# A fused attention and feed-forward kernel: weight tiles decoded in pairs, in alternating operations, one pair a unit behind the gate's second remainder

## The chip, the cores and the metric

The kernel runs on one core of a Trainium2 chip. The metric is the device time of one execution in microseconds. Before the change it is 1063.06 us, the median of three runs (1061.4 to 1063.42).

The core has five engines with a queue each, and a queue runs in order: TensorE (PE in the rows; its weight loads are PEld), VectorE (DVE), ScalarE (ACT), GpSimd (POOL) and SyncE (SP), which here only issues DMAs. TensorE writes to PSUM, which has eight banks; the other engines evacuate them.

## The reference

Attention with a causal mask and a memory term, over 4 batches, 8 heads, 576 positions and 64 channels, gives 2304 tokens of 512 channels. Two feed-forward blocks follow:

```python
def _moe_ref(x, w_in, w_out):          # d_ff = 2048
    h = x @ w_in
    sp = np.where(h > 20.0, h, np.log1p(np.exp(np.minimum(h, 20.0))))
    g = h * np.tanh(sp)
    return (g @ w_out).astype(np.float32)

def _moe2_ref(x, w1, w2, w3, w_out):   # d_ff = 1024
    a = x @ w1
    b = x @ w2
    h = a * b @ w3
    return (h @ w_out).astype(np.float32)
```

The weights lie in DRAM as 64-bit floats.

## The kernel before

**Precision.** Each float32 operand of the feed-forward blocks is held as a rounded high part and a remainder, so a product is three matmuls: high by high, high by remainder, remainder by high.

**Decoding weights.** A weight tile of 128 by 512 is loaded as pairs of 32-bit words into a buffer `draw` (512 KB, line 94) and made into float32 by `decode` (lines 91 to 109): six VectorE operations on the whole tile, each on the result of the one before, at lines 99, 100, 101, 103, 104 and 105, and one GpSimd addition at line 108, which leaves the float32 tile in a buffer `da`. Then either `split_w` (line 114) rounds it on GpSimd (`pool_round`, line 64) and subtracts for the remainder (line 67, on GpSimd), both into the weight slot, or `split_to_dram` (line 119) writes both parts over the `draw` buffer and stores them to DRAM (line 126). The number of `draw` and `da` buffers is set by `decoder(stack, raw, n)`: 3 and 2 in the gated block, 2 and 2 from its last quarter on.

**Stages.** Attention comes first, some 0 to 290 us, for 16 pairs of heads; ten tiles are decoded beside it. The gated block (`_moe_ref`) follows in 24 units `u = (g, n)`: four quarters g of the 2048 columns, six chunks n of 384 tokens, loop at line 607. A unit does `emit_h(u)` (line 410 on: 48 matmuls into four PSUM banks, tanh, arctan and sine on ScalarE, and the gate product at line 443 on VectorE), then `emit_x2` of the unit before (line 523: 48 matmuls into the three `X` banks in four groups of 12; each group is evacuated by VectorE at line 537 or added to `x2` at line 539), then `split_y(u)` (line 446: high parts `gh` on ScalarE, two remainders `gl` on VectorE), whose VectorE instructions `tc.issue_after` queues behind the last evacuation of `emit_x2`. In the quarters before the last, the unit then decodes tiles: of the next quarter's weights (`load_quarter`, eight tiles, into one of two slots `wq0` and `wq1`), and of `predecode`, which puts the halves of three later weights into DRAM (16 tiles). Two `load_quarter` tiles come in units 0 and 1 of a quarter and one in each other; one `predecode` tile comes in most units from 1 on (lines 628, 629).

In the last quarter `fold` (line 544) multiplies w3 by the last output weight, in 16 steps that each decode one tile of w3 and transpose it on TensorE (line 563); its buffers take the place of the decoder's. The last stage (`emit_ab`, `emit_out`, about 755 us to the end) needs the second halves of w1 and w2: eight tiles decoded by `second_half` (line 149), two beside the last `emit_x2` and two behind each of the steps k = 0, 1 and 2.

**Order.** The program is written as generators; `steps(gen, n)` runs n steps of one. A planner then orders each engine's queue by simulated times, earlier in the program first among what is ready. An instruction without an edge to others may so move past what stands before it in the program.

Of the kernel before, what the change touches and what calls it, by code (L numbers as in the profile page):

```python
# [2 lines left out]

# [18 lines left out]
def fused_kernel(ctx: ExitStack, tc, q, k, v, M_prev, z_prev, beta, w_in, w_out, w1, w2, w3, w_out2, out):  # L22
# [65 lines left out]
    def dec_tile(tag):  # L88
        return dec["pool"].tile([128, dec["w"]], F32, tag=tag, name=tag, bufs=dec["n"])

    def decode(src):

        r = dec["pool"].tile([128, dec["w"], 2], I32, tag="draw", name="draw", bufs=dec["raw"])
        dm(out=r.rearrange("p n t -> p (n t)"), in_=src)
        lw, hw = r[:, :, 0], r[:, :, 1]
        a = dec_tile("da")
        ai, e = a.bitcast(I32), lw.bitcast(F32)
        V = nc.vector
        V.tensor_scalar(out=ai, in0=hw, scalar1=0x7FFFFFFF, scalar2=None, op0=ALU.bitwise_and)  # L99
        V.tensor_scalar(out=a, in0=a, scalar1=2.0 ** -15, scalar2=122879.9921875, op0=ALU.max, op1=ALU.min)  # L100
        V.tensor_scalar(out=ai, in0=ai, scalar1=3, scalar2=0x3FFFFFF8,  # L101
                        op0=ALU.logical_shift_left, op1=ALU.bitwise_and)
        V.scalar_tensor_tensor(out=ai, in0=hw, scalar=-0x40000000, in1=ai, op0=ALU.bitwise_and, op1=ALU.bitwise_or)  # L103
        V.tensor_scalar(out=hw, in0=ai, scalar1=-0x800000, scalar2=None, op0=ALU.bitwise_and)  # L104
        V.scalar_tensor_tensor(  # L105
            out=e, in0=lw.bitcast(U32), scalar=2.0 ** -52, in1=hw.bitcast(F32), op0=ALU.mult, op1=ALU.mult
        )
        nc.gpsimd.tensor_tensor(out=a, in0=a, in1=e, op=ALU.add)  # L108
        return a, r.rearrange("p n t -> p (n t)").bitcast(F32)

    def words(w, r0, c0):
        return w[r0:r0 + 128, c0:c0 + dec["w"]].bitcast(I32)

    def split_w(hi, lo, src):
        a, _ = decode(src)
        pool_round(hi, a)
        sub(lo, a, hi, nc.gpsimd)

    def split_to_dram(dst, src):

        a, r = decode(src)
        w = dec["w"]
        hi, lo = r[:, 0:w], r[:, w:2 * w]
        pool_round(hi.bitcast(F32R), a)
        nc.gpsimd.tensor_tensor(out=lo.bitcast(F32R), in0=a, in1=hi, op=ALU.subtract)
        dm(out=dst.rearrange("i p c -> p i c"), in_=r.rearrange("p (i c) -> p i c", i=2))


    ident = const.tile([128, 128], F32, name="ident")
    make_identity(nc, ident)  # L130
# [12 lines left out]
    def predecode():  # L143
        for w, wd in ((w_out2, o2_dram), (w1, w1_dram), (w2, w2_dram)):
            for c in range(w.shape[0] // 128):
                split_to_dram(wd[:, 128 * c:128 * c + 128, 0:WN], words(w, 128 * c, 0))
                yield

    def second_half(t):
        for i, w in ((1, w2), (0, w1)):  # L150
            for c in range(KD):
                split_w(t[:, i, 0, c], t[:, i, 1, c], words(w, 128 * c, WN))
                yield

    xl = {}

# [9 lines left out]
    def load_quarter(g):  # L166
        t = (wq if g % 2 == 0 else w2q[0]).tile([128, 2, KD + KQ, FQ], F32R, tag=f"wq{g % 2}", name="wqt")
        wts[g] = t
        for c in range(KD):
            split_w(t[:, 0, c], t[:, 1, c], words(w_in, 128 * c, FQ * g))  # L170
            yield
        for c in range(KQ):
            split_w(t[:, 0, KD + c], t[:, 1, KD + c], words(w_out, FQ * g + 128 * c, 0))
            yield

    w2q = [None]

# [268 lines left out]
    def split_y(u, y):  # L446
        gg = []
        for i in range(2):
            gh = wps[0].tile([128, 2, CH], F32R, tag="gh", name="gh", bufs=2)
            gl = wps[0].tile([128, 2, CH], F32R, tag="gl", name="gl", bufs=2)  # L450
            nc.scalar.copy(out=gh, in_=y[i])  # L451
            sub(gl, y[i], gh)
            gg.append((gh, gl))
        gt[u] = gg

    wk = ExitStack()
    wps = [None]
# [8 lines left out]
    for p in range(NPAIR + 1):  # L466

        now, old, new = p < NPAIR, p > 0, p + 1 < NPAIR
        if old:
            ensure_x((p - 1) // (2 * NP))  # L470
        if not now:
            ek.close()
            wps[0] = wk.enter_context(tc.tile_pool(name="wp", bufs=1, side="right"))
        if now:
            s_blocks(p, (3,))
        if old:
            for i in (4, 2, 3):
                pt_g(p - 1, i)
        if new:
            prep_qk(p + 1)  # L480
        if now:
            s_blocks(p, (2,))
            if p == 0:
                prep_phi(0)
            s_blocks(p, (0, 1))
        if p + 2 < NPAIR:
            load_pair(p + 2)
        if old:
            pt_g(p - 1, 5)
            if not now:  # L490
                steps(lq0, 100)
                split_y((0, 0), emit_h((0, 0)))
            pt_g(p - 1, 6)
        if now:
            normed(p, [(i, e) for e in range(2) for i in range(4)])
            pt_g(p, 1)
        if 2 <= p < 12:
            steps(background, 1)
# [45 lines left out]
    def fold():  # L544
        o2 = wq.tile([128, 2, 8, DM], F32R, tag="wq0", name="o2")
        oh, ol = o2[:, 0], o2[:, 1]
        for h in range(2):
            for i in range(2):
                dm(
                    out=f(o2[:, i, 4 * h:4 * h + 4]),  # L550
                    in_=o2_dram[i, 512 * h:512 * h + 512].rearrange("(k p) f -> p k f", p=128),
                )

        held = None
        po = None
        fp = fpool[0]
        for s in range(2 * (FF2 // 128) + 1):
            pt = None
            if s < 2 * (FF2 // 128):
                a, _ = decode(words(w3, 128 * (s // 2), 512 * (s % 2)))  # L560
                pt = psF()
                for j in range(4):
                    nc.tensor.transpose(pt[:, 128 * j:128 * j + 128], a[:, 128 * j:128 * j + 128], ident)
            if held is not None:
                n, th, tl = held
                m, g = n // 2, n % 2
                if g == 0:
                    po = psF()
                for j in range(4):
                    kk = 4 * g + j  # L570
                    mm(po, th[:, j], oh[:, kk], kk == 0, False)
                    mm(po, th[:, j], ol[:, kk], False, False)
                    mm(po, tl[:, j], oh[:, kk], False, kk == 7)
                if g == 1:
                    for h in range(2):
                        cs = slice(256 * h, 256 * h + 256)
                        wo = fp.tile([128, 256], F32, tag="wo", name="wo", bufs=1)
                        nc.scalar.copy(out=wo, in_=po[:, cs])
                        dm(out=w_dram[128 * m:128 * m + 128, cs], in_=wo)
            held = None  # L580
            if pt is not None:
                th = fp.tile([128, 4, 128], F32R, tag="w3h", name="w3h", bufs=1)
                tl = fp.tile([128, 4, 128], F32R, tag="w3l", name="w3l", bufs=1)
                pw = pt.rearrange("p (a b) -> p a b", b=128)
# [15 lines left out]
        return t  # L600

    folding = fold()
    pre0 = iter(())
    nextq = iter(())
    prev = None
    w1t, w2t = [None, None], [None, None]
    for u in [(g, n) for g in range(NQ) for n in range(NCH)]:
        g, n = u
        last = g == NQ - 1
        if u not in gt:  # L610
            if last and fpool[0] is None:
                steps(nextq, 100)
                steps(pre, 100)
# [5 lines left out]
            w_slot(0)  # L619
        if prev is not None:  # L620
            with tc.issue_after(emit_x2(prev, folding if last and n > 0 else pre0)):
                split_y(u, y)
        if last and n == 0:
            steps(folding, 1)
        if not last:
            if n == 0:
                nextq = load_quarter(g + 1)
            steps(nextq, 2 if n < 2 else 1)
            steps(pre, 1 if n in (1, 3, 4, 5) or (g < 2 and n == 2) else 0)
        prev = u  # L630
    NM = FF2 // 128

# [2 lines left out]
    for s in range(4):  # L635
# [1 line left out]
            out=f(wft[:, 1, 2 * s:2 * s + 2]),  # L637
            in_=w_dram[256 * s:256 * s + 256, :].rearrange("(k p) f -> p k f", p=128),
        )
    rest = second_half(w_slot(1))  # L640
    emit_x2(prev, rest)
    wk.close()


# [59 lines left out]
    split_x2(0)  # L704
    for k, (c, m) in enumerate(work):
        if k == 4:
            steps(rest, 100)
            fk.close()
            late = ctx.enter_context(tc.tile_pool(name="late", bufs=1))
            x2s = late.tile([128, 2, KD, 512], F32R, name="x2s")  # L710
# [46 lines left out]
```

## Time and profile before

| | |
|---|---|
| median of three runs | 1063.06 us |
| profiled execution, its own time | 1061.77 us |
| its span | 1060.0 us |
| TensorE busy | 1021.9 us (96%) |
| VectorE busy | 662.6 us (63%) |
| ScalarE busy | 502.5 us (47%) |
| GpSimd busy | 349.4 us (33%) |

The profiled execution lies 1.3 us under the median and within the three runs; 1.8 us of it lie outside the span. Times of rows are counted from the span's start. A busy time is the sum of an engine's instructions in a stretch. Matmuls overlap, so the length of one says less than the distance between two or the time of a row of them.

### The profile page before, as it was taken

How to read it: one execution, taken by the hardware profiler on the slowest of the kernel's cores; microseconds unless marked ns; L12 is line 12 of the kernel's file. 1: busy time of each engine (PE TensorE's matmuls, PEld its weight loads, DVE VectorE, ACT ScalarE, POOL GpSimd, SP SyncE). 2: the span in 40 equal slices, each digit the busy share in tenths (PEclk: the TensorE clock that was granted, in tenths of full speed). 3: DMA queues.
4: the chain of work that ended last, by engine and by line, in shares of the span. 5: the costliest groups of instructions: out<-in, count | busy, mean ns of one | idle time of the engine just before them, and what ended most of it. 6: DMA issues, size and time to landing. Idle time of an engine off the chain costs nothing.

```text
span 1060.0 us, 15074 instructions
## 1 busy us (share of the span) xinstructions
PE 1021.9 (96%) x5552; PEld 852.3 (80%) x5552; DVE 662.6 (63%) x1364; ACT 502.5 (47%) x1016; POOL 349.4 (33%) x345
## 2 busy tenths in 40 slices
PE   7999999999989899799979999999989999999998
PEld 4555655656789899799979999999868888888897
DVE  5999998854699847994887566566994112121111
ACT  4777867866654565346545643544323122211212
POOL 6776666632265515541553112011550000000000
PEclk9999999999999899999999999999999999999999
DMA  6434344310223301331132156222410010100101
GB/s 149 112 96 114 92 106 112 88 31 3 100 99 121 120 20 45 135 130 50 40 124 96 41 204 228 75 80 70 159 60 1 1 40 1 41 0 1 41 1 60
DMA packets 93626, 81.73 MB, mean 77 GB/s; under 512 B 68720, under 2 KB 72816, under 8 KB 93552
## 3 DMA queue, kind: packets, MB, share of 16 engines
q1 hardware_dynamic: 93552, 80.76, 24.6%
q8 instruction: 44, 0.72, 0.3%
q14 instruction: 30, 0.25, 0.1%
HBM read 65.54 MB, written 15.20 MB: 76 GB/s over the span
## 4 chain that ended last, share of the span: by engine, by line
PE 71%; DVE 18%; POOL 4%; issue 2%; DMA 2%; ACT 2%; SPq 1%; POOLq 0%; DVEq 0%; ACTq 0%
PE psX L61 27%; PE psA L61 25%; PE psF L61 12%; PE psF L385 4%; PE psX L266 2%; DVE da L99 2%; DVE da L100 2%; DVE da L103 2%; DVE draw L104 2%; DVE draw L105 2%; DVE da L101 2%; DVE y L443 1%; POOL da L108 1%; DVE gl L67 1%; POOL wqt L67 1%
## 5 line engine op out<-in xcount | busy, mean ns | idle before, releaser
L61 PE MATMUL psX<-gh,wqt 128*128 128x384 f32 x768 | 200.2, 342 | 17.0 <-DVE x L539 11.4
L108 POOL TENSOR_TENSOR da<-da,draw 128x512 f32<-128x512 f32 x72 | 106.2, 1476 | 289.3 <-DVE draw L105 250.9
L61 PEld LDWEIGHTS psX<-gh,wqt 128*128 128x128 f32 x768 | 141.3, 192 | 20.4 <-DVE x L539 12.8
L61 PE MATMUL psX<-gl,wqt 128*128 128x384 f32 x384 | 130.1, 341 | 0.8 <-DVE gl L67 0.6
L61 PE MATMUL psA<-xt,wqt 128*128 128x384 f32 x624 | 117.3, 338 | 2.1 <-DVE y L443 2.1
L61 PEld LDWEIGHTS psA<-xt,wqt 128*128 128x128 f32 x624 | 110.4, 190 | 3.9 <-DVE y L443 2.4
L337 ACT ACTIVATE s<-s,acc 128x384 f32<-128x384 f32 (+3 forms) x144 | 85.0, 595 | 37.5 <-DVE acc L332 21.0
L61 PE MATMUL psA<-x2h,w12t 128*128 128x512 f32 (+1 forms) x288 | 80.7, 355 | 4.2 <-POOL w12t L64 3.5
L451 ACT CAST gh<-y 128x768 fp32r<-128x768 f32 x48 | 40.1, 837 | 92.0 <-PE psX L61 46.6
L61 PE MATMUL psX<-wft,room 128*128 128x512 f32 x336 | 82.6, 390 | 0.0
L99 DVE TENSOR_SCALAR da<-draw 128x512 int32<-128x512 int32 x72 | 44.5, 619 | 53.8 <-issue 12.9
L332 DVE CUSTOM_DVE_ANT_0 s<-psA,mask 128x512 f32<-128x512 f32 (+2 forms) x144 | 64.9, 478 | 19.8 <-PE psA L61 17.2
L681 ACT COPY bs<-psA 128x512 f32<-128x512 f32 (+1 forms) x40 | 21.8, 544 | 113.5 <-PE psA L61 105.5
L61 PE MATMUL psX<-pt,raw 128*64 128x64 f32 (+4 forms) x576 | 75.0, 328 | 0.0
L61 PEld LDWEIGHTS psX<-gl,wqt 128*128 128x128 f32 x384 | 73.6, 192 | 1.6 <-DVE gl L67 1.4
L61 PE MATMUL psA<-kt,qt 64*128 64x384 f32 (+3 forms) x256 | 71.0, 485 | 3.4 <-DVE acc L332 2.8
L61 PE MATMUL psF<-xt,wqt 128*128 128x384 f32 x408 | 74.0, 335 | 0.0
L61 PEld LDWEIGHTS psX<-wft,room 128*128 128x128 f32 x336 | 62.6, 188 | 12.7
L387 ACT COPY pt<-psF 128x512 f32<-128x512 f32 (+1 forms) x112 | 59.0, 544 | 26.9 <-PE psF L385 23.4
L61 PEld LDWEIGHTS psF<-xt,wqt 128*128 128x128 f32 x408 | 70.9, 188 | 0.4 <-DVE y L443 0.3
L61 PE MATMUL psA<-x2s,w12t 128*128 128x512 f32 x288 | 67.9, 389 | 0.0
L682 DVE TENSOR_TENSOR bs<-bs,psA 128x512 f32<-128x512 f32 (+1 forms) x20 | 12.7, 633 | 87.3 <-PE psA L61 87.3
(117 smaller groups left out, 2022.6 us busy)
## 6 DMA issues: line engine op xcount, KB each, us to landing
draw<-in_moe_w_dram SPq DMA_DIRECT2D x32, 512.0 KB, 3.7
draw<-in_moe_w_out_dram SPq DMA_DIRECT2D x24, 512.0 KB, 3.7
draw<-in_moe_w_in_dram SPq DMA_DIRECT2D x16, 512.0 KB, 3.9
out_dram<-ob SPq DMA_DIRECT2D x18, 256.0 KB, 2.0
raw<-in_q_dram SPq DMA_DIRECT2D x32, 128.0 KB, 2.7
raw<-in_k_dram SPq DMA_DIRECT2D x32, 128.0 KB, 3.2
raw<-in_v_dram SPq DMA_DIRECT2D x32, 128.0 KB, 2.7
o_dram<-draw SPq DMA_DIRECT2D x8, 512.0 KB, 2.8
```

Source lines behind the costliest of these rows:

```text
L61: nc.tensor.matmul(o, lhsT=l, rhs=r, start=start, stop=stop)
L67: return (eng or nc.vector).tensor_tensor(out=dst, in0=src, in1=f(hi), op=ALU.subtract)
L99: V.tensor_scalar(out=ai, in0=hw, scalar1=0x7FFFFFFF, scalar2=None, op0=ALU.bitwise_and)
L100: V.tensor_scalar(out=a, in0=a, scalar1=2.0 ** -15, scalar2=122879.9921875, op0=ALU.max, op1=ALU.min)
L101: V.tensor_scalar(out=ai, in0=ai, scalar1=3, scalar2=0x3FFFFFF8, op0=ALU.logical_shift_left, op1=ALU.bitwise_and)
L108: nc.gpsimd.tensor_tensor(out=a, in0=a, in1=e, op=ALU.add)
L332: nc.vector.tensor_tensor_reduce(out=s, in0=o, in1=m, op0=ALU.add, op1=ALU.min, scale=-scale, scalar=init, accum_out=a,)
L337: nc.scalar.activation(out=s, in_=s, func=AF.Exp, scale=-1.0, bias=a, accum_out=r)
L385: nc.tensor.transpose(o[:, 128 * x:128 * x + 128], src[:, 128 * jb:128 * jb + 128], ident)
L387: nc.scalar.copy(out=t[:, 0:n], in_=o[:, 0:n])
L451: nc.scalar.copy(out=gh, in_=y[i])
L681: nc.scalar.copy(out=bs, in_=pb)
```

## The change

`decode` takes a list of sources and gives the six VectorE operations for all of them in turns: the first operation of each tile, then the second of each, and so on; the GpSimd addition and what follows is done tile by tile. `load_quarter`, `predecode` and `second_half` now yield jobs, a source and what is to be done with the decoded tile, and `run(jobs, n)` decodes n of them together. In the gated block a unit runs one pair behind `split_y`, which returns its second remainder; `tc.issue_after(split)` queues the pair's VectorE instructions behind it. Unit 0 of a quarter takes two `predecode` tiles (four in unit (0, 0)), units 1 to 3 take two tiles of the next quarter, units 4 and 5 one of each kind. `second_half` goes in pairs at its old places, the first pair at the start of the last `emit_x2`. In attention a single tile is run at a time as before, and so in `fold`.

```diff
+    def decode(srcs):
+        V = nc.vector
+        ts = []
+        for src in srcs:
+            r = dec["pool"].tile([128, dec["w"], 2], I32, tag="draw", name="draw", bufs=dec["raw"])
+            dm(out=r.rearrange("p n t -> p (n t)"), in_=src)
+            a = dec_tile("da")
+            ts.append((r[:, :, 0], r[:, :, 1], a, a.bitcast(I32), r.rearrange("p n t -> p (n t)").bitcast(F32)))
+        for lw, hw, a, ai, _ in ts:
+            V.tensor_scalar(out=ai, in0=hw, scalar1=0x7FFFFFFF, scalar2=None, op0=ALU.bitwise_and)
+        for lw, hw, a, ai, _ in ts:
+            V.tensor_scalar(out=a, in0=a, scalar1=2.0 ** -15, scalar2=122879.9921875, op0=ALU.max, op1=ALU.min)
...
+        for lw, hw, a, ai, _ in ts:
+            nc.gpsimd.tensor_tensor(out=a, in0=a, in1=lw.bitcast(F32), op=ALU.add)
+            yield a, _
+
+    def run(jobs, n):
+
+        jobs = list(islice(jobs, n))
+        for (a, r), (_, done) in zip(decode([src for src, _ in jobs]), jobs):
+            done(a, r)
+
+    def by_two(jobs):
+        for _ in range(4):
+            run(jobs, 2)
+            yield
...
-            sub(gl, y[i], gh)
+            r = sub(gl, y[i], gh)
             gg.append((gh, gl))
         gt[u] = gg
+        return r.ins
...
             with tc.issue_after(emit_x2(prev, folding if last and n > 0 else pre0)):
-                split_y(u, y)
+                split = split_y(u, y)
+        with tc.issue_after(split):
+            if u == (0, 0):
+                run(pre, 2)
+            if n == 0:
+                run(pre, 2)
+            elif not last:
+                run(nextq if n < 4 else chain(islice(nextq, 1), islice(pre, 1)), 2)
         if last and n == 0:
             steps(folding, 1)
-        if not last:
-            if n == 0:
-                nextq = load_quarter(g + 1)
-            steps(nextq, 2 if n < 2 else 1)
-            steps(pre, 1 if n in (1, 3, 4, 5) or (g < 2 and n == 2) else 0)
+        if not last and n == 0:
+            nextq = load_quarter(g + 1)
...
-    rest = second_half(w_slot(1))
-    emit_x2(prev, rest)
+    rest = by_two(second_half(w_slot(1)))
+    emit_x2(prev, islice(rest, 1))
...
         if k < 3:
-            steps(rest, 2)
+            steps(rest, 1)
```

## Rows read from the trace of the kernel before

**Rows 1.** Windows: stretch, length, busy time and instructions by engine, clock, DMA.
```profile
293.80:593.30 299.50, 279.81 (x1562) 276.46 (x1562) 242.83 (x385) 159.40 (x216) 133.67 (x110) 0.97 0.26 90
...
310.00:320.00 10.00, 7.39 (x41) 7.07 (x42) 9.86 (x15) 6.54 (x10) 6.71 (x6) 1.00 0.43 159
...
350.00:360.00 10.00, 5.74 (x23) 5.42 (x22) 9.38 (x14) 3.25 (x5) 6.95 (x7) 0.73 0.47 157
```
**Rows 2.** Chain that ended last: start, length, engine, tile, line, count.
```profile
355.86 4.21 PE psX L61 x12
...
368.88 8.32 PE psX L61 x48
```
**Rows 3.** Groups, TensorE, 293.8 to 593.3: busy, mean ns, idle before, releasers.
```profile
L61 PE MATMUL psX<-gh,wqt 128*128 128x384 f32 x544 | 142.2, 343 | 16.8 <-DVE x L539 11.4 <-DVE x L537 5.4
...
L61 PE MATMUL psA<-xt,wqt 128*128 128x384 f32 x361 | 67.4, 339 | 2.1 <-DVE y L443 2.1
```
**Rows 4.** Timeline, TensorE: start, length, line, instruction, count, idle before with releaser.
```profile
355.86 1.01 PE L61 MATMUL psX<-gh,wqt 128*128 128x384 f32 x2 [4.26 <-DVE x L537]
```
**Rows 5.** Timeline, VectorE, 350 to 356 us.
```profile
350.49 1.51 DVE L99 TENSOR_SCALAR da<-draw 128x512 int32<-128x512 int32 x1 [1.18 <-POOL draw L125]
...
355.26 0.55 DVE L537 COPY x<-psX 128x384 f32<-128x384 f32 x1
```
**Rows 6.** Timeline, VectorE: two tiles in turns (583 us), one alone (734 us).
```profile
583.74 0.76 DVE L101 TENSOR_SCALAR da<-da 128x512 int32<-128x512 int32 x2
584.41 1.28 DVE L103 SCALAR_TENSOR_TENSOR da<-draw,da 128x512 int32<-128x512 int32 x2
585.62 0.76 DVE L104 TENSOR_SCALAR draw<-da 128x512 int32<-128x512 int32 x2
...
734.28 0.43 DVE L101 TENSOR_SCALAR da<-da 128x512 int32<-128x512 int32 x1
734.74 0.69 DVE L103 SCALAR_TENSOR_TENSOR da<-draw,da 128x512 int32<-128x512 int32 x1
735.47 0.43 DVE L104 TENSOR_SCALAR draw<-da 128x512 int32<-128x512 int32 x1
```
**Rows 7.** Timeline, GpSimd, 345 to 395 us.
```profile
345.10 2.90 POOL L108 TENSOR_TENSOR da<-da,draw 128x512 f32<-128x512 f32 x1 [6.10 <-DVE draw L105]
...
350.42 1.29 POOL L108 TENSOR_TENSOR da<-da,draw 128x512 f32<-128x512 f32 x1
...
352.56 1.31 POOL L67 TENSOR_TENSOR wqt<-da,wqt 128x512 fp32r<-128x512 f32 x1
...
394.01 1.90 POOL L64 TENSOR_SCALAR wqt<-da 128x512 fp32r<-128x512 f32 x2 [24.04 <-PE psX L61]
```
**Rows 8.** Timeline, VectorE: remainders of two units; second tile of the second half.
```profile
394.36 2.35 DVE L67 TENSOR_TENSOR gl<-y,gh 128x768 fp32r<-128x768 f32 x2
...
593.95 1.82 DVE L67 TENSOR_TENSOR gl<-y,gh 128x768 fp32r<-128x768 f32 x2
...
745.90 1.50 DVE L99 TENSOR_SCALAR da<-draw 128x512 int32<-128x512 int32 x1 [0.64 <-PE psF L563]
```
**Rows 9.** DMA issues: tile, queue, count, KB each, median us to landing.
```profile
draw<-in_moe_w_dram SPq DMA_DIRECT2D x32, 512.0 KB, 3.7
...
o_dram<-draw SPq DMA_DIRECT2D x8, 512.0 KB, 2.8
```
**Rows 10.** Timeline, TensorE: the fold's first transposes and first product.
```profile
605.76 1.03 PE L563 MATMUL psF<-ident,da 128*128 128x128 f32 x8
...
619.82 0.39 PE L61 MATMUL psF<-o,w3h 128*128 128x512 f32 x1
```
**Rows 11.** Timeline, GpSimd: first addition and last remainder of the second half.
```profile
743.72 1.30 POOL L108 TENSOR_TENSOR da<-da,draw 128x512 f32<-128x512 f32 x1 [5.56 <-DVE draw L105]
...
795.40 1.29 POOL L67 TENSOR_TENSOR w12t<-da,w12t 128x512 fp32r<-128x512 f32 x1
```
**Rows 12.** Groups, TensorE, whole span: a group of the last stage.
```profile
L61 PE MATMUL psA<-x2h,w12t 128*128 128x512 f32 (+1 forms) x288 | 80.7, 355 | 4.2 <-POOL w12t L64 3.5 <-ACT bs L681 0.6
```

More of the change, by code (lines that the diff above doesn't have):

```diff
@@ L1 @@
 from contextlib import ExitStack
-from itertools import chain
+from itertools import chain, islice
 import concourse.bass as bass
@@ L89, in dec_tile @@
         return dec["pool"].tile([128, dec["w"]], F32, tag=tag, name=tag, bufs=dec["n"])
[L91 to L97, printed above, removed]
-        V = nc.vector
[L99 to L109, printed above, removed]
@@ new lines, in decode @@
+    def decode(srcs):
+        V = nc.vector
+        ts = []
[9 more added lines that the diff above has]
+        for lw, hw, a, ai, _ in ts:
+            V.tensor_scalar(out=ai, in0=ai, scalar1=3, scalar2=0x3FFFFFF8,
+                            op0=ALU.logical_shift_left, op1=ALU.bitwise_and)
+        for lw, hw, a, ai, _ in ts:
+            V.scalar_tensor_tensor(
+                out=ai, in0=hw, scalar=-0x40000000, in1=ai, op0=ALU.bitwise_and, op1=ALU.bitwise_or
+            )
+        for lw, hw, a, ai, _ in ts:
+            V.tensor_scalar(out=hw, in0=ai, scalar1=-0x800000, scalar2=None, op0=ALU.bitwise_and)
+        for lw, hw, a, ai, _ in ts:
+            V.scalar_tensor_tensor(
+                out=lw.bitcast(F32), in0=lw.bitcast(U32), scalar=2.0 ** -52, in1=hw.bitcast(F32),
+                op0=ALU.mult, op1=ALU.mult,
+            )
+        for lw, hw, a, ai, _ in ts:
+            nc.gpsimd.tensor_tensor(out=a, in0=a, in1=lw.bitcast(F32), op=ALU.add)
+            yield a, _
@@ L111, in words, with to_split, done @@
+    def run(jobs, n):
[6 more added lines that the diff above has]
+            yield
     def words(w, r0, c0):
         return w[r0:r0 + 128, c0:c0 + dec["w"]].bitcast(I32)
[L114 to L126, printed above, removed]
+    def to_split(hi, lo):
+        def done(a, r):
+            pool_round(hi, a)
+            sub(lo, a, hi, nc.gpsimd)
+        return done
@@ L129, in fused_kernel, with to_dram, done @@
+    def to_dram(dst):
+        def done(a, r):
+            w = dec["w"]
+            hi, lo = r[:, 0:w], r[:, w:2 * w]
+            pool_round(hi.bitcast(F32R), a)
+            nc.gpsimd.tensor_tensor(out=lo.bitcast(F32R), in0=a, in1=hi, op=ALU.subtract)
+            dm(out=dst.rearrange("i p c -> p i c"), in_=r.rearrange("p (i c) -> p i c", i=2))
+        return done
     ident = const.tile([128, 128], F32, name="ident")
@@ L145, in predecode @@
             for c in range(w.shape[0] // 128):
-                split_to_dram(wd[:, 128 * c:128 * c + 128, 0:WN], words(w, 128 * c, 0))
-                yield
+                yield words(w, 128 * c, 0), to_dram(wd[:, 128 * c:128 * c + 128, 0:WN])
     def second_half(t):
@@ L151, in second_half @@
             for c in range(KD):
-                split_w(t[:, i, 0, c], t[:, i, 1, c], words(w, 128 * c, WN))
-                yield
+                yield words(w, 128 * c, WN), to_split(t[:, i, 0, c], t[:, i, 1, c])
     xl = {}
@@ L169, in load_quarter @@
         for c in range(KD):
-            split_w(t[:, 0, c], t[:, 1, c], words(w_in, 128 * c, FQ * g))
-            yield
+            yield words(w_in, 128 * c, FQ * g), to_split(t[:, 0, c], t[:, 1, c])
         for c in range(KQ):
-            split_w(t[:, 0, KD + c], t[:, 1, KD + c], words(w_out, FQ * g + 128 * c, 0))
-            yield
+            yield words(w_out, FQ * g + 128 * c, 0), to_split(t[:, 0, KD + c], t[:, 1, KD + c])
     w2q = [None]
@@ L490, in fused_kernel @@
             if not now:
-                steps(lq0, 100)
-                split_y((0, 0), emit_h((0, 0)))
+                run(lq0, 100)
+                split = split_y((0, 0), emit_h((0, 0)))
             pt_g(p - 1, 6)
@@ L497, in fused_kernel @@
         if 2 <= p < 12:
-            steps(background, 1)
+            run(background, 1)
         if now:
@@ L559, in fold @@
             if s < 2 * (FF2 // 128):
-                a, _ = decode(words(w3, 128 * (s // 2), 512 * (s % 2)))
+                (a, _), = decode([words(w3, 128 * (s // 2), 512 * (s % 2))])
                 pt = psF()
@@ L602, in fused_kernel @@
     folding = fold()
-    pre0 = iter(())
-    nextq = iter(())
+    pre0 = nextq = iter(())
     prev = None
@@ L611, in fused_kernel @@
             if last and fpool[0] is None:
-                steps(nextq, 100)
-                steps(pre, 100)
                 dk.close()
@@ L706, in fused_kernel @@
         if k == 4:
-            steps(rest, 100)
             fk.close()
```

## Prediction

> **What bounds the kernel now.** I read the busy shares by stage first, then TensorE's waits inside the worst stage, then the queue of the engine waited for. From about 800 us to the end the chain of waits is TensorE without a gap, and the attention stage before 250 us is full as well; neither holds anything that this change touches. The stage between them is the gated feed-forward: 24 units (g, n), each one `emit_h` (48 matmuls) and one `emit_x2` of the unit before (48 matmuls). From the first `emit_x2` at 293.8 us to the first `emit_h` of the last quarter at 593.3 us TensorE is busy 279.81 of 299.50 us at a mean granted clock of 0.97, VectorE 242.83 [rows 1]. Where nothing disturbs it, 48 matmuls take 8.32 us [rows 2]. The stretch holds 16 `emit_h` and 17 `emit_x2`, by the loop at line 607, so its work is 33 x 8.32 = 274.6 us, and 299.5 - 274.6 = 24.9 us are lost.
>
> The loss is not spread. In 368.88 to 377.20 us TensorE runs at full rate [rows 2], in 350 to 360 it is busy 5.74 us with the clock at 0.73 [rows 1]. The waits named are 16.8 us for VectorE's evacuations of `emit_x2` and 2.1 us for the gate product [rows 3], 18.9 together; the other 6.0 us is mostly the clock after such gaps: 12 matmuls took 4.21 us behind the longest one [rows 2], where 48 in 8.32 us make 2.08. That longest gap is 4.26 us for an evacuation [rows 4], which VectorE ran at 355.26, after a row of weight decode operations that began at 350.49 with one of 1.51 us [rows 5]. Undisturbed operations of that kind take 0.43 [rows 6]. The long one ends at 352.00, just behind a GpSimd addition from 350.42 with 1.29 us, and the addition before that took 2.90 us [rows 7]: the decode of one tile runs beside the GpSimd part of another, each stretches the other, and evacuations and gate products stand behind them in VectorE's queue.
>
> Why it crowds: in the first unit of a quarter the two tiles of the next quarter are decoded at once, but their rounding waits 24.04 us for `emit_x2` to leave the weight slot [rows 7]. Both `da` buffers are held meanwhile, and the other 11 tiles of the quarter fall into five units.
>
> **The change, part by part.**
>
> *Queueing behind the second remainder.* A unit is 2 x 8.32 = 16.64 us. In the quiet unit that starts at 368.88 + 8.32 = 377.20 [rows 2] the two remainders begin at 394.36 with 2.35 us for both [rows 8]: they end 19.5 us after the unit's start, 2.9 us into the next one. A pair decodes in 12 operations: where two tiles take turns, the next two start 0.67 us after two `tensor_scalar` (583.74 to 584.41) and 1.21 after two `scalar_tensor_tensor` (584.41 to 585.62) [rows 6], so 4 x 0.67 + 2 x 1.21 = 5.1 us. It lies at 2.9 to 8.0 us of the unit, while TensorE does `emit_h` and asks VectorE for nothing. `emit_x2` begins at 8.32; it has three banks, so its fourth group at 8.32 + 3 x 2.08 = 14.6 us is the first that needs an evacuation. Cover of the pair: 14.6 - 8.0 - 0.55 for the evacuation [rows 5] = 6 us. A GpSimd tile is 350.42 to 352.56 + 1.31 = 3.45 us [rows 7], a pair 6.9; it starts when the first tile leaves VectorE, at some 7.4, and ends at 14.3. The next pair wants its buffers at 19.5. So GpSimd works while VectorE handles PSUM and the gate, no longer beside another decode. 24.9 us is the ceiling of this part.
>
> *Spread over the units.* Two tiles a unit, four in (0, 0), none written to a weight slot in the first unit of a quarter: the 24 us wait [rows 7] has nothing left to hold. The same 38 tiles are decoded, with as many loads, stores and GpSimd operations. SP's queue: a load takes 3.7 us, a store 2.8 [rows 9]. With three `draw` buffers the second load of a pair needs the first tile of the pair before. If that tile goes to DRAM: 7.4 + 3.4 + 2.8 + 3.7 = 17.3 us, under 19.9; if an addition slips between, 18.7. That covers a pair a unit. In (0, 0) two pairs follow each other, and the second waits for the first's store, until some 15 us after it; its work then falls on the first unit's gate and remainders. No row shows this crowding; the nearest is the idle of the same place before, 2.61 us in 310 to 320 [rows 1]. Bounds 0 to 4 us; I take 2, since it happens once.
>
> *The fold's start.* The last pair now stands behind the remainders of unit (2, 5), which end at 595.8 [rows 8]; 5.1 us of decode, 6.9 of GpSimd and 2.8 of store reach 610.6, and only then may the fold's buffers take the old pool's place: load 3.7, a pair 5.1, an addition 1.3, so 620.7, against its transposes at 605.76 before [rows 10]. But the first product of the fold came at 619.82 before too [rows 10], and behind the transposes lie only a rounding and a remainder of some 1.3 us: 622.5. TensorE has `emit_h` and `emit_x2` of the last quarter to fill with. Bounds 0 to 3 us, taken 1.
>
> *The second half of w1 and w2.* Here the fold's pool is kept: two `draw`, two `da`. Before, GpSimd added the first tile at 743.72 and began the last remainder at 795.40, and TensorE waited 4.2 us in that stage, 3.5 of it for such tiles [rows 11, 12]. In pairs, the second load must wait for the second addition: pair chain 4.2 us to the first tile's end, 4.1 to 4.8 on GpSimd to the second addition's end, 3.7 of load and 0.4 of issue, 12.4 to 13.1 a pair. The second tile began at 745.90, when the last w3 tile had left its buffer [rows 8], and the first pair can hardly begin earlier; 745.9 + 3 x 12.8 + 4.2 + 6.9 = 795.4 for the last tile, against 796.7. So nothing, with -4 (the waits vanish) to +8 (2 us of other remainders inside each of four pairs) as ends.
>
> *Alternating itself.* A tile decoded alone starts its next operation 0.46 us after a `tensor_scalar` and 0.73 after a `scalar_tensor_tensor` (734.28 to 734.74; 734.74 to 735.47), against 0.34 and 0.60 in turns [rows 6]: 4 x 0.46 + 2 x 0.73 = 3.3 us for one, 6.6 for two, against 5.1. In the units that 1.5 us is covered and counted at nothing. The Trainium skill (VectorE: DVE Perf Modes, The DRAIN you can't avoid) says that the next operation does not start until the pipe is empty, whether or not a semaphore stands between, by which alternation would give nothing. The rows differ from that, 0.34 against 0.46 us, and the sum goes by the rows.
>
> **Sum.** -24.9 + 2 + 1 + 0 = -21.9 us. The profiled execution took 1061.77 us (span 1060.0), which gives 1039.9; the median 1063.06 is 1.3 above it and would give 1041.2. I forecast 1040.5.
>
> **Rivals.**
>
> *Partial gain.* Evacuations still stand behind decodes, since the planner, whose times need not hold on the chip, may let a pair slip into the next `emit_x2`. For it: stretching moves work later than planned, as at 350 us [rows 5]. Against: 6 us of cover. Half of 24.9 back: 1049, between 1045 and 1056.
>
> *The second half decides.* Pairs there cost 8 to 12 us, since both buffers are handed over at once and nothing is decoded meanwhile: 1048 to 1052. For it: two buffers. Against: the same cadence by the sum above.
>
> *The head of the queue blocks: slower.* An operation of a pair that waits for its load or its `da` holds VectorE's queue, and with it evacuations and gate products. It costs from the point where a pair ends later than 14.0 us of its unit, 6 us late; at 24.9 / 17 = 1.5 us a unit the gain is gone. With 2.6 us a unit, the idle of 310 to 320 [rows 1], 17 units cost 44 us: 1082. The longest addition is 2.90 against 1.30 [rows 7]; a GpSimd pair stretched in that measure takes 15.4 us and ends at 22.8, 3 us late, still covered. So little speaks for it.
>
> *Turns give nothing.* If tiles in turns took as long as alone, four pairs of the second half would take 4 x 1.5 = 6 us more: 1046.5. The rows of two tiles in turns speak against it [rows 6].
>
> *No effect.* The planner already alternates where two tiles are ready [rows 6], and decodes that TensorE did not wait for gain nothing: 1061 to 1065.
>
> **Chances and range.** Forecast (1033 to 1046) 0.63; partial gain 0.13; second half 0.09; turns give nothing 0.02; no effect 0.05; slower 0.08. Low end: 24.9 + 4 gained, 1033. High end: 24.9 less 4, 3 and 8 leaves 10 gained, 1052, which also takes in the second rival and most of the first: 1053. Outside are the last two rivals and a little of the first. About 0.2% (2 us) is what a measurement here can tell from no change: faster 0.88, same 0.04, slower 0.08.
>
> **What would show it.** Right: TensorE over 97% busy at clock 1.00 from `emit_x2` (0, 0) to the last quarter, that stretch near 277 us; no wait for an evacuation over 1 us; the first operation of each pair right behind two remainders; decode operations near 0.43 us; no GpSimd rounding that waits 20 us. Wrong: gaps that end on an evacuation in every unit (the blocked queue), waits for `w12t` of over 5 us in all (the second half), a gap at the fold's first transposes, or a full stage with a time above 1050.

## The result and the profile after

The changed kernel takes 1036.17 us (median) against 1063.12 us for the kernel before, timed in turn with it: a ratio of 0.9745, 95% interval 0.9726 to 0.9764. The forecast was 1040.5 us in a range of 1033 to 1053. The profiled execution took 1036.43 us, its span is 1034.6 against 1060.0 us, so 25.4 us less. One of the four runs of the kernel after (2003.24 us) and one of an experiment below (3478.26 us) were slow runs, which the ratios leave out.

Where they went is read from two markers in each trace. The first `emit_x2` starts at 293.81 us before and 293.50 after; the first `emit_h` of the last quarter at 593.28 and 567.22. The gated stage between them shrank from 299.47 to 273.72 us, by 25.75; what follows it grew from 466.72 to 467.38. All of the gain lies in the stage that the prediction named, and nothing that counts was given back.

Windows of the kernel after, to be read against [rows 1] (stretch, length, busy time and instructions of PE, PEld, DVE, ACT and POOL, clock, DMA share, GB/s):

```profile
293.80:567.20 273.40, 270.93 (x1560) 269.97 (x1559) 189.89 (x371) 161.19 (x216) 116.57 (x104) 1.00 0.27 93
310.00:320.00 10.00, 7.99 (x44) 7.67 (x45) 9.68 (x17) 6.54 (x10) 6.31 (x5) 1.00 0.54 174
350.00:360.00 10.00, 10.00 (x60) 10.00 (x59) 7.57 (x16) 4.92 (x8) 3.06 (x3) 1.00 0.07 26
```

TensorE is busy 99% of the stage at full clock, where it was 93% at 0.97. VectorE's records there are 371 operations in 189.89 us, 0.51 us each, where 385 took 242.83, 0.63 each: the decodes are no longer stretched. (Most of the 14 fewer are the last pair's twelve, which now start at 569.63 us, behind the stretch.) The window at 310 us is the one place that is not mended. TensorE's groups in that stretch, answering to [rows 3] (busy us, mean ns, idle before, releaser):

```profile
L61 PE MATMUL psX<-gh,wqt 128*128 128x384 f32 x544 | 137.9, 334 | 0.0
L61 PE MATMUL psX<-gl,wqt 128*128 128x384 f32 x272 | 90.7, 335 | 1.1 <-DVE gl L67 1.1
...
L61 PE MATMUL psA<-xt,wqt 128*128 128x384 f32 x360 | 65.3, 335 | 1.4 <-DVE y L463 1.4
```

The 16.8 us for evacuations are 0; what is left is one wait of 1.1 us and one of 1.4, both between 308 and 318 us. A quiet unit on VectorE, answering to [rows 5, 6, 8] (start, length, line, instruction, count, idle before):

```profile
384.86 1.82 DVE L67 TENSOR_TENSOR gl<-y,gh 128x768 fp32r<-128x768 f32 x2
386.59 0.76 DVE L101 TENSOR_SCALAR da<-draw 128x512 int32<-128x512 int32 x2
387.26 0.76 DVE L103 TENSOR_SCALAR da<-da 128x512 f32<-128x512 f32 x2
387.93 0.76 DVE L105 TENSOR_SCALAR da<-da 128x512 int32<-128x512 int32 x2
388.60 1.29 DVE L108 SCALAR_TENSOR_TENSOR da<-draw,da 128x512 int32<-128x512 int32 x2
389.81 0.76 DVE L112 TENSOR_SCALAR draw<-da 128x512 int32<-128x512 int32 x2
390.48 1.28 DVE L114 SCALAR_TENSOR_TENSOR draw<-draw 128x512 f32<-128x512 uint32 x2
394.78 0.55 DVE L560 TENSOR_TENSOR x<-x,psX 128x384 f32<-128x384 f32 x1 [3.02 <-PE psX L61]
```

The pair stands right behind the two remainders, takes 5.2 us, and VectorE then waits 3 us for TensorE. GpSimd's part of the pair falls into that pause, on GpSimd's timeline:

```profile
391.30 2.88 POOL L119 TENSOR_TENSOR da<-da,draw 128x512 f32<-128x512 f32 x2 [10.07 <-DVE draw L114]
394.14 1.20 POOL L64 TENSOR_SCALAR draw<-da 128x512 fp32r<-128x512 f32 x2
```

Two additions take 2.88 us, where one took 2.90 in [rows 7], and no rounding waits 24 us any more.

### The profile page after: what moved, and what is told of

Its sections match the earlier page's. It is cut to its first block, busy times and chain, and to the rows that moved or that the text cites. A ratio compares the mean times of both kernels' runs of the same rounds, so it can differ in the third digit from the quotient of the medians.

```text
span 1034.6 us, 15072 instructions
## 1 busy us (share of the span) xinstructions
PE 1014.0 (98%) x5552; PEld 847.1 (82%) x5552; DVE 615.5 (59%) x1364; ACT 505.1 (49%) x1016; POOL 337.9 (33%) x345
## 4 chain that ended last, share of the span: by engine, by line
PE 86%; DVE 6%; ACT 3%; SPq 2%; DMA 2%; issue 1%; POOL 1%; POOLq 0%; DVEq 0%; ACTq 0%
PE psX L61 34%; PE psA L61 29%; PE psF L61 16%; PE psF L405 5%; PE psX L286 2%; SPq L268 1%; ACT y L459 1%; DVE da L105 1%; PE psF L584 1%; DVE s L347 1%; ACT L456 0%; DMA draw<-in_moe_w_dram 0%; DVE da L103 0%; DVE gl L67 0%; DMA wft<-w_dram 0%
## 5 line engine op out<-in xcount | busy, mean ns | idle before, releaser
L119 POOL TENSOR_TENSOR da<-da,draw 128x512 f32<-128x512 f32 x72 | 104.1, 1455 | 331.4 <-DVE draw L114 255.9
L61 PE MATMUL psX<-gh,wqt 128*128 128x384 f32 x768 | 196.1, 335 | 0.2
L61 PEld LDWEIGHTS psX<-gh,wqt 128*128 128x128 f32 x768 | 138.6, 188 | 1.5 <-DVE y L463 0.5
L61 PE MATMUL psA<-xt,wqt 128*128 128x384 f32 x624 | 115.0, 336 | 1.4 <-DVE y L463 1.4
L560 DVE TENSOR_TENSOR x<-x,psX 128x384 f32<-128x384 f32 x72 | 39.6, 549 | 54.1 <-PE psX L61 53.9
L405 PEld LDWEIGHTS psF<-ident,s 128*128 128x128 f32 x400 | 45.3, 141 | 26.1 <-ACT phi L330 10.6
```

What stands on the lines that cost most here:

```text
L61: nc.tensor.matmul(o, lhsT=l, rhs=r, start=start, stop=stop)
L119: nc.gpsimd.tensor_tensor(out=a, in0=a, in1=lw.bitcast(F32), op=ALU.add)
L405: nc.tensor.transpose(o[:, 128 * x:128 * x + 128], src[:, 128 * jb:128 * jb + 128], ident)
L560: r = nc.vector.tensor_tensor(out=d, in0=d, in1=o, op=ALU.add)
```

## The experiments

All times are medians, all ratios against the kernel before, timed in turn, with a 95% interval. Theory: the place in the queue makes the gain, since a pair that is kept together behind the remainders meets neither evacuations nor GpSimd's part of another tile. Rivals: the even spread of two tiles a unit makes it; or the turns do. The turns were not taken out of the program without another edit; the second experiment shows that the planner takes ready tiles in turns by itself.

**Undo the place, keep the spread and the turns.**

```diff
-        with tc.issue_after(split):
+        if True:
```

> The kernel after without the edge that queues a pair behind the gate's second remainder; the spread of the tiles over the units and the turns stay. Theory A (the place in VectorE's queue brings the gain): decodes slip in front of evacuations and gate products again, TensorE waits 10 us or more between the first emit_x2 and the last quarter, 1048 to 1060 us. Rival B (the spread brings it, since no tile holds its buffers through the 24 us wait for the weight slot): 1034 to 1040 us, as the kernel after with 1036.

Measured: 1063.65 us, ratio 1.0014 [1.0005, 1.0023]. The whole gain is gone, and TensorE's waits in the stage are those of before (waited for: us in all, times, longest):

```profile
PE psX L61 <- DVE x L560: 11.2, 4, 3.9
PE psX L61 <- DVE x L558: 5.1, 3, 4.3
PE psA L61 <- DVE y L463: 2.1, 1, 2.1
PE psX L61 <- DVE gl L67: 0.9, 1, 0.9
```

The even spread does nothing without the place. Nor does it end the wait for the weight slot, by which the rival went: GpSimd still waits 7.29 us for it, and later 23.59.

```profile
503.35 1.91 POOL L64 TENSOR_SCALAR wqt<-da 128x512 fp32r<-128x512 f32 x2 [23.59 <-PE psX L61]
```

**Do the place alone**, in the kernel before, with its own spread and tile after tile in the program.

```diff
...
+            with tc.issue_after(split):
-            steps(nextq, 2 if n < 2 else 1)
-            steps(pre, 1 if n in (1, 3, 4, 5) or (g < 2 and n == 2) else 0)
+                steps(nextq, 2 if n < 2 else 1)
+                steps(pre, 1 if n in (1, 3, 4, 5) or (g < 2 and n == 2) else 0)
```

> The kernel before with its own spread of the tiles (two of the next quarter's in the first unit), only their VectorE instructions queued behind the second remainder of their unit. Theory A: most of the gain, 1036 to 1045 us, with GpSimd still waiting some 20 us for the weight slot in each quarter. Rival B: the buffers are held through that wait, the third tile of the second unit waits at the head of VectorE's queue, 1048 to 1063 us.

Measured: 1039.91 us, ratio 0.979 [0.9775, 0.9804]. Of the 27 us that the change brings, one edge in one queue brings some 22. One evacuation wait of 2.7 us is left, at 330 to 400 us. GpSimd waits for no weight slot, though the spread is the old one and the expectation had some 20 us of it in each quarter. The turns come without being written:

```profile
370.55 0.75 DVE L99 TENSOR_SCALAR da<-draw 128x512 int32<-128x512 int32 x2
371.22 0.75 DVE L100 TENSOR_SCALAR da<-da 128x512 f32<-128x512 f32 x2
```

The kernel after is 4 to 5 us faster still, but not by the spread of this stage in the main. The stage takes 274.85 us here, 1.1 more than in the kernel after, and what follows it 470.83, some 3.5 more. This kernel also lacks the pairs of the second half; which part of the 3.5 us they make was not tried.

**Take the turns away**, by queueing the second tile of a pair behind the first one's last VectorE operation.

```diff
...
+            if i and dec["raw"] == 3:
+                es.enter_context(tc.issue_after(dec["end"].ins))
...
```

> The kernel after with the second tile of each pair of the gated block queued behind the first one's last VectorE operation, so that the two can't take turns. A pair then needs 6.6 us of VectorE for 5.1. Theory A: covered by the 6 us between the pair and the first evacuation that TensorE needs, 1035 to 1038 us. Rival C (the turns carry a part of the gain): 1.5 us in each of 17 units, up to 25 us more, 1045 to 1061.

Measured: 1042.84 us, ratio 0.9818 [0.9803, 0.9833], some 7 us slower than the kernel after and between the two expectations. Its VectorE timeline shows why a pair without turns is longer than the prediction's 6.6 us:

```profile
389.39 0.42 DVE L101 TENSOR_SCALAR da<-draw 128x512 int32<-128x512 int32 x1
389.85 0.43 DVE L103 TENSOR_SCALAR da<-da 128x512 f32<-128x512 f32 x1
...
391.96 0.69 DVE L114 SCALAR_TENSOR_TENSOR draw<-draw 128x512 f32<-128x512 uint32 x1
392.57 0.42 DVE L101 TENSOR_SCALAR da<-draw 128x512 int32<-128x512 int32 x1
393.02 1.42 DVE L103 TENSOR_SCALAR da<-da 128x512 f32<-128x512 f32 x1
...
395.23 1.66 DVE L108 SCALAR_TENSOR_TENSOR da<-draw,da 128x512 int32<-128x512 int32 x1
...
397.99 0.55 DVE L564 TENSOR_TENSOR x<-x,psX 128x384 f32<-128x384 f32 x1
```

The first tile takes 3.2 us, but its GpSimd part then runs beside the second tile, which takes 5.4: 8.6 in all against 5.2. In the quiet units this is covered: from 400 to 550 us TensorE is busy 150.00 of 150.00 us. It is paid where a unit is not quiet, 1.8 us of idle in 330 to 400 and 1.9 us at the fold's first transposes; the stage grows by 2.7 us and what follows it by 3.1.

**One pair less in unit (0, 0)**, done in the attention stage instead.

```diff
-        if 2 <= p < 12:
+        if 2 <= p < 14:
...
-            if u == (0, 0):
-                run(pre, 2)
```

> The kernel after with two more tiles decoded in attention (background to p = 13) and so one pair less in unit (0, 0). If the two waits left in the stage (1.10 us for a remainder and 1.36 for a gate product, 308 to 318 us) come from the four tiles of the first unit, they go, and the time falls by 2 to 3 us: 1033 to 1034.5. If they come from the stage's start as such, they stay and the time is 1036; if attention has no room for two more tiles it loses some 3 us for each: 1038 to 1042.

Measured: 1036.6 us, ratio 0.9754 [0.9737, 0.977], the same as the kernel after. The two waits are gone (TensorE busy 103.30 of 103.30 us in 296.7 to 400), so the second pair of unit (0, 0) was their cause. The 1033 to 1034.5 us expected from that did not come. But the first `emit_x2` starts at 296.7 us instead of 293.5: two decodes more beside attention make TensorE busy 48.41 of 50 us in 200 to 250, where it had no gap. By the last quarter 0.1 us of the gain is left (567.1 against 567.2), and the rest of the run took 1.7 us longer.

**The two tiles as third tiles of later units.** In one kernel in units (1, 3) and (2, 3), in another in (0, 4) and (1, 4):

```diff
-            if u == (0, 0):
-                run(pre, 2)
+            if u in ((0, 4), (1, 4)):
+                run(pre, 1)
```

> The kernel after, with one pair instead of two in unit (0,0); the two tiles that it decodes no more are done as a third tile in units (1,3) and (2,3), not in the attention stage as in the experiment before. Theory: the 2.5 us of waits at 308 to 318 us vanish, the third tile of 3.3 us fits under the 6 us of cover, and the attention stage is as it was: 1034.0, 2.4 us under the kernel after. Rival (a third tile must wait for a da buffer until GpSimd has finished the pair's first tile, and holds VectorE's queue, the evacuations with it): 2 to 5 us in each of two units, so 1036 to 1044.

> The kernel after, with one pair instead of two in unit (0,0); the two tiles are done as a third tile in units (0,4) and (1,4), earlier than in the experiment with (1,3) and (2,3), which gained 2.5 us at the start and lost 2.4 us at the fold's first transposes. If that loss came from the third tile in the last quarter before the fold: no wait at the fold, 1033 to 1034.5. If it came from the place of the fold in the queues, whatever happens before it: 1036 again.

Measured: 1035.88 us, ratio 0.9735 [0.9719, 0.9751], and 1034.97 us, ratio 0.9747 [0.9734, 0.976]. In both the waits at 308 to 318 us vanish. In the first TensorE waits 2.4 us for the fold's first `da`; in the second it does not, which fits a late third tile pushing the fold's decodes, but the kernel with 0.67 us more a pair (below) waits 1.7 us there without a third tile. The second just misses its 1033 to 1034.5 us and is no faster than the kernel after beyond the intervals: in its last stage the waits for `w12t`, `w3l` and `bs` make 6.8 us against 5.1 there. No version tried beats the kernel after by more than can be measured.

**The pair ahead of the remainders.** The same pair in the same unit, one place earlier: behind the last evacuation, with the remainders behind the pair.

```diff
...
-        if prev is not None:
-            with tc.issue_after(emit_x2(prev, folding if last and n > 0 else pre0)):
-                split = split_y(u, y)
-        with tc.issue_after(split):
+        at = emit_x2(prev, folding if last and n > 0 else pre0) if prev is not None else split
+        with tc.issue_after(at):
...
+        if prev is not None:
+            with tc.issue_after(at if last and n > 0 else dec["end"].ins):
+                split = split_y(u, y)
```

> The kernel after, with the pair queued one place earlier: behind the last evacuation of the emit_x2 before, and the two remainders behind the pair's last VectorE operation. If it is the place behind the second remainder that counts: the remainders, which ended at 386.6 in the steady unit, end at 391.7, 0.8 us before the emit_x2 that needs them starts at 392.5; any stretched pair (a VectorE operation beside a GpSimd one) is then paid in full, 1 to 2 us in every unit, 1053 to 1070, as waits for gl. If it counts only that no decode stands between the evacuations of emit_x2: within 2 us of the kernel after in the steady units, some 2 to 4 us in the first units of the quarters, 1036 to 1041.

Measured: 1064.2 us, ratio 1.001 [0.9999, 1.0021]. The gain is gone again, with other waits: 18.5 us for `gl` (7 times, the longest 10.9), 2.7 for `y`, none for an evacuation. It is not a cost of every unit, as the first expectation had it: from 330 to 400 us TensorE is busy 69.81 of 70 us. Nor is it the 1036 to 1041 us of the second. It is paid in a few units: 11.5 us of idle from 293.5 to 330 us, where the pairs of units (0, 0) and (0, 1) crowd ahead of a remainder, 3.9 from 420 to 430 and 4.8 from 500 to 570. At the first place no load is waited for; two tiles are decoded one behind the other beside GpSimd, from 308.96 to 319.57 us, and the remainder comes after them (first VectorE, then TensorE):

```profile
316.84 1.63 DVE L108 SCALAR_TENSOR_TENSOR da<-draw,da 128x512 int32<-128x512 int32 x1
...
320.58 0.69 PE L61 MATMUL psX<-gl,wqt 128*128 128x384 f32 x1 [10.86 <-DVE gl L67]
```

VectorE at the second place:

```profile
416.03 0.43 DVE L105 TENSOR_SCALAR da<-da 128x512 int32<-128x512 int32 x1
420.78 0.43 DVE L101 TENSOR_SCALAR da<-draw 128x512 int32<-128x512 int32 x1 [4.32 <-DMA draw<-in_moe_w_in_dram]
...
425.47 0.98 DVE L114 SCALAR_TENSOR_TENSOR draw<-draw 128x512 f32<-128x512 uint32 x1
426.37 2.91 DVE L67 TENSOR_TENSOR gl<-y,gh 128x768 fp32r<-128x768 f32 x2
```

A tile whose load has not landed holds VectorE's queue for 4.32 us with the remainders behind it, and another for 2.57 us before 526.73. This is the prediction's blocked queue, on the other side of the remainders. In the kernel after the corresponding loads are issued at 399.47 us, after the stores of the pair before, and the pair starts at 403.23: no wait of VectorE for a load is recorded in the stage, and behind the pair VectorE pauses 2.86 us before the next evacuation, at 411.42. What stands behind the pair there can wait; the remainders, one place earlier, cannot.

**Longer pairs: how much cover is there?** The first operation of each tile is done 2, 4, 6 and 13 times in units (0, 1) to (2, 5), which adds 0.67, 2.0, 3.4 and 8.2 us a pair.

```diff
...
-            V.tensor_scalar(out=ai, in0=hw, scalar1=0x7FFFFFFF, scalar2=None, op0=ALU.bitwise_and)
+            for _ in range(dec.get("again", 1)):
+                V.tensor_scalar(out=ai, in0=hw, scalar1=0x7FFFFFFF, scalar2=None, op0=ALU.bitwise_and)
...
```

> The kernel after, with the first decode operation of each tile done six times instead of once in the units (0,1) to (2,5) (17 pairs; the result is the same): 10 operations more a pair at about 0.34 us, so a pair takes some 8.5 us instead of 5.2. VectorE is then busy about 14.2 of the 16.64 us of a unit. Theory (6 us of cover behind the remainders): TensorE does not notice, the gated stage stays within 2 us of 273.7 us, the time between 1035 and 1039. Rival (what VectorE does more is paid by TensorE, in whole or part, because evacuations stand right behind the pair): 17 x 3.4 = 58 us in whole, 1094; half of it, 1065.

> The same with thirteen times: 24 operations more a pair, some 8.2 us, so a pair takes about 13.3 us and ends some 7.4 us into emit_x2. Theory (cover 6 us, and then the head of the queue blocks): the fourth group of emit_x2 waits for its evacuation, about 8.2 - 6 = 2 us a unit and the slowed clock behind it, and VectorE has about 19 us of work for a unit of 16.64: 17 units x 2 to 3 us, so 1070 to 1087, with a wait for an evacuation in every unit. Rival (VectorE's total alone counts, the place does not): (19 - 16.64) x 17 = 40 us, 1076, but with the waits spread over gate products and evacuations. If it stays under 1045, the cover was far larger than 6 us.

> The kernel after, with the first decode operation of each tile done twice in the units (0,1) to (2,5): 0.67 us more a pair. In the queues written for it the two tiles of a pair still stand together between the remainders and the next evacuation, but for the first unit. If what counts is that a pair stays together: within 1.5 us of the kernel after, 1035 to 1038. If each us of VectorE's time in a unit costs TensorE what it did in the experiment with 3.4 us more (33 us for 17 x 3.4 = 58 us, 0.57 a us): 17 x 0.67 x 0.57 = 6.5 us, 1043.

> The same with four times: 2.0 us more a pair, well under the 6 us of cover; VectorE has some 12.8 us of work in a unit of 16.64. In the queues written for it the two tiles of a pair slip apart in most units of the first quarter and stand between the evacuations. If the cover of 6 us were usable: 1036 to 1039. If a pair that is broken up is what costs: decodes stretched to over 1 us beside GpSimd and waits for evacuations, 10 to 25 us, 1046 to 1061. By the 0.57 of the experiment with 3.4 us more: 17 x 2.0 x 0.57 = 20 us, 1056.

| added a pair | time, us | ratio to before | TensorE busy 293.5 to 400 (106.5) | 400 to 500 (100) |
|---|---|---|---|---|
| 0 (the kernel after) | 1036.17 | 0.9745 [0.9726, 0.9764] | 104.03 | 100 |
| 0.67 us | 1037.97 | 0.9777 [0.9763, 0.979] | 103.96 | 100.00 |
| 2.0 us | 1051.22 | 0.9905 [0.9891, 0.9918] | 97.90 | 100.00 |
| 3.4 us | 1069.55 | 1.006 [1.0045, 1.0075] | 97.33 | 94.66 |
| 8.2 us | 1172.67 | 1.1016 [1.0996, 1.1035] | 102.33 | 80.94 |

The row with 2.0 us shows both sides at once. Its windows, first in the first quarter, then in the second:

```profile
340.00:380.00 40.00, 36.61 (x201) 35.97 (x200) 39.45 (x65) 19.57 (x28) 17.59 (x16) 0.96 0.20 67
...
440.00:480.00 40.00, 40.00 (x233) 40.00 (x232) 31.47 (x69) 23.33 (x31) 16.55 (x16) 1.00 0.24 81
```

The kernel after in the same stretches:

```profile
340.00:380.00 40.00, 40.00 (x232) 40.00 (x231) 27.06 (x57) 23.85 (x33) 18.54 (x18) 1.00 0.23 79
...
440.00:480.00 40.00, 40.00 (x232) 40.00 (x232) 23.87 (x49) 24.01 (x33) 18.65 (x18) 1.00 0.23 80
```

From 400 us on the 2 us are covered in full: VectorE is 7.6 us busier in these 40 us (4.8 would be 2.0 us a unit) and TensorE notices nothing. In the first quarter VectorE is busy 39.45 of 40 us for 65 instructions, against 31.47 for 69. There the two tiles of a pair stand apart in the queue, from unit (0, 1) on, where the second pair of (0, 0) was still pending. With 3.4 us added VectorE is over 98% busy in every 40 us from 300 to 560. VectorE of that kernel:

```profile
403.42 1.41 DVE L104 TENSOR_SCALAR da<-da 128x512 f32<-128x512 f32 x1
404.86 0.73 DVE L106 TENSOR_SCALAR da<-da 128x512 int32<-128x512 int32 x1
405.62 1.66 DVE L109 SCALAR_TENSOR_TENSOR da<-draw,da 128x512 int32<-128x512 int32 x1
...
408.39 0.55 DVE L561 TENSOR_TENSOR x<-x,psX 128x384 f32<-128x384 f32 x1
408.86 2.04 DVE L102 TENSOR_SCALAR da<-draw 128x512 int32<-128x512 int32 x2
```

and GpSimd beside the first of them:

```profile
403.12 1.42 POOL L120 TENSOR_TENSOR da<-da,draw 128x512 f32<-128x512 f32 x1 [8.58 <-DVE draw L115]
404.63 0.68 POOL L64 TENSOR_SCALAR draw<-da 128x512 fp32r<-128x512 f32 x1
405.39 1.34 POOL L149 TENSOR_TENSOR draw<-da,draw 128x512 fp32r<-128x512 f32 x1
```

One tile is decoded beside the GpSimd part of the other (1.41 for 0.42 us), and decodes stand between evacuations. VectorE does not catch up before the stage ends. Evacuation waits are back at 16.2 us. Of the 33 us lost, 22.5 lie in the stage, 1.3 a unit for 3.4 added: the first `emit_h` of the last quarter starts at 590.15 us, 296.24 behind the first `emit_x2`. The other 10 lie behind it. The expectation from 6 us of cover, 1035 to 1039, was wrong; that for 2.0 us was wrong too, and the one by broken pairs held in its time (1046 to 1061), but with 6.1 us of waits for evacuations where it had 10 to 25. Of the 15 us lost with 2.0 us more, 8.9 lie in the stage (282.58 us against 273.72), 6 of them idle time before 400 us, and in its last stage TensorE waits 4.2 us for `wft` and 4.1 for `bs`, which it does not in the kernel after; what that has to do with the pairs was not tried. With 8.2 us TensorE waits 52.6 us for `wqt` tiles that come too late and 24.0 for `y`, while VectorE is busy 97.88 of 100 us from 400 to 500: decoding itself has become the bound. Neither expectation had the waits for weight tiles, and both (at most 1087 us) fell far short.

## Why the prediction was right

**The bound and the mechanism: right.** The loss lay in the gated stage, evacuations stood behind stretched decodes, and the place in the queue mends it: undone, the whole loss comes back; done alone, 22 of 27 us are gained.

**Why it crowds: wrong for the first quarter, open for the others.** The prediction put the crowding on the 24 us wait for the weight slot. That wait begins at 369.97 us (394.01 - 24.04), behind two of the evacuation waits, the 4.26 us before 355.86 [rows 4] and this one of the kernel before:

```profile
336.00 0.61 PE L61 MATMUL psX<-gh,wqt 128*128 128x384 f32 x2 [1.17 <-DVE x L537]
```

It was also not the even spread that ended the wait, as the part-by-part account had it: the spread without the place keeps it, the place with the old spread has none. What share of the later quarters' loss came from it no run separates.

**The ceiling of 24.9 us: a little small.** The stage gave 25.75 and still has some 2.5 us of idle in unit (0, 0). The term took 33 rows of 48 matmuls as its work, 274.6 us. But the stretch of [rows 1] holds 1562 recorded matmuls and that of after 1560, where 33 x 48 = 1584: about half a row lies outside or is unrecorded. Without the two waits the stage would be 273.72 - 2.5 = 271.2 us, so the loss was about 28 us. The clock's part was undersized with it: the 18.9 us of named waits leave some 9, not 6.0, and TensorE's busy time in the stage fell by 8.9 us (279.81 to 270.93).

**Crowding in unit (0, 0): right**, 2 us taken, 2.46 measured, and at its place: a kernel without the second pair has no wait there. After, decodes of 1.42 and 1.67 us at 303 and 305 us and remainders of 3.08 at 308.80 show it.

**The fold: the cost right in size, the time line wrong.** One us was taken for a start that moves from 12.5 to 27 us behind the last quarter's start. The first transposes come 29.1 us behind it (596.35 us) and the first product 35.0 (602.26) instead of 26.5, which is 6 us later than the 29 us of the sum. TensorE had other work: it is busy 49.86 of 50 us from 600 to 650. So nothing that shows instead of 1. Pairs without turns, a third tile or 0.67 us more a pair do cost there: 1.9, 2.4 and 1.7 us.

**The second half: nothing, as taken, but by luck.** From its first addition to its last remainder GpSimd needs 53.9 us after (717.42 to 771.35) and 53.0 before [rows 11]. The waits that answer to [rows 12]:

```profile
L61 PE MATMUL psA<-x2h,w12t 128*128 128x512 f32 (+1 forms) x288 | 81.1, 357 | 2.9 <-POOL w12t L64 2.8
```

The pairs slip apart here, since the second load lands later, and are decoded much as before; the chain of 12.8 us a pair was not what was seen, so that its result agrees is luck. `w3l` is waited for 2.3 us instead of 1.4.

**Turns in the units counted at nothing: half right.** Their 1.5 us a pair are covered in quiet units. But without them the second tile runs beside the first one's GpSimd part, which costs 3.4 us more a pair, not 1.5, and some 7 us in the whole. The rival that turns give nothing falls by the rows, 5.2 us a pair against 6.6. The time does not decide it: its 6 us were to come from the second half, where the pairs slipped apart. A tile alone in that kernel starts its next operation 0.46 us after a `tensor_scalar` (389.39 to 389.85) and 0.73 after a `scalar_tensor_tensor`, as in [rows 6]. The prediction read in the Trainium skill (VectorE: DVE Perf Modes, The DRAIN you can't avoid) that turns would give nothing, and went by the rows. The same section of the Trainium skill also says that a next operation that is not held starts earlier. The prediction left that out; the operations in turns do start earlier, after 0.34 and 0.60 us.

**Six us of cover: wrong as a free margin.** The sum of positions is true of a pair that stays together, as the second quarter with 2.0 us more shows. It left out that the order of the queue is planned by when tiles are ready, so that a longer pair can be broken up; that the buffers are handed on with little to spare may have a part in it, which was not tried. The same omission is in the blocked queue's price, "from the point where a pair ends later than 14.0 us": with 3.4 us more the pairs would by that sum end at some 11.4, and the gain was gone.

**Rivals.** Partial gain (1049) and no effect did not occur. The blocked queue did not occur in the kernel after, but does one place earlier in the queue, in two units. There a load comes late because its `draw` buffer must first be stored, the cycle that the prediction put at 17.3 us of a unit's 19.9, and TensorE waits 3.88 and 2.23 us. The larger wait of that kernel, 10.86 us, is not this rival but stretched decodes ahead of a remainder.

## What to carry to other kernels

Work that is off the critical path but shares an engine with it wants a place in that engine's queue, not only a rate: here an edge behind the last operation that TensorE is waiting for gave 22 of 27 us, and the same work one place earlier or unplaced gave none. Ask what stands behind that work if one of its inputs is late, and leave the longest pause there. A margin summed up from a quiet unit holds only while the order holds: test it by making the work longer. Look at the first unit too, where a backlog starts: here it was gone by 400 us with 2.0 us more a pair, and with 3.4 it was not gone by the stage's end.

## What the runs showed of the hardware

That VectorE and GpSimd slow each other on tiles of 128 by 512 was in the rows of before; how much of a whole stage it makes was not expected. A `tensor_scalar` of 0.42 us takes 1.4 beside a GpSimd addition, a `scalar_tensor_tensor` of 0.69 takes 1.66 beside a GpSimd subtraction, and two additions beside the `gl` remainders took 4.62 us (at 386.56 us, with the pair ahead of the remainders) against 2.88 in VectorE's pause. With the two engines at work at different times, VectorE's mean operation in the stage fell from 0.63 to 0.51 us. The granted clock was lower where TensorE had waited longest: 0.97 in the stage before, 1.00 after, and 0.80 from 420 to 430 us of the kernel with the pair ahead of the remainders, where TensorE waited 3.88 us.
